# Gated attention and an MLP mixer in one kernel: z^T from overlapping transposes, the second token weight kept in row order, stores on the GpSimd queue

## The chip, the cores and the metric

The kernel runs on one core of one Trainium2 chip. A core has a matmul engine (TensorE, PE in the profile), three engines for elementwise work (VectorE is DVE, ScalarE is ACT, GpSimd is POOL), and SyncE (SP), which here only issues DMAs. SP and POOL each issue to a DMA queue of their own, in order; an instruction that waits holds all that stands behind it on its engine. The metric is the device time of one execution in microseconds; lower is better.

## The reference

There are 8 batches of 3008 rows. The first stage is attention with a squared ReLU and a gate, the second a mixer over tokens and then over channels. `z` is the query and the key at once, so the scores are symmetric.

```python
scores = z @ z^T / S                     # S = 3008, z: [S, 64]
attn   = maximum(scores, 0) ** 2
x      = u * (attn @ v)                  # u, v: [S, 256]
h      = maximum(x^T @ w_tok1, 0) @ w_tok2     # w_tok1: [S, 256], w_tok2: [256, S]
x2     = x + h^T
out    = x2 + maximum(x2 @ w_ch1, 0) @ w_ch2   # w_ch1: [256, 1536]
```

Inputs and the output are float32; the kernel computes in bfloat16 with float32 sums.

## The kernel before, in words

**Tiles.** The 3008 rows of a batch are 24 tiles of 128 (the last has 64 rows), in 6 groups of 4 (`GK`); `q` counts groups as queries, 512 columns (`QW`), and `g` as keys. Rows are loaded so that a partition takes neighbouring rows of DRAM (`rows_of`: row p*t + i, t = 4 or 3, goes to partition p, tile i). All that is indexed by a row must follow this order.

**Attention.** `score_run` (L399) multiplies z^T with itself. A score needs only 64 rows of PE's array, so two of them run at once, in the lower and the upper half; for this z^T stands in both halves (`zTs[b]`, partitions 0 to 63 and again 64 to 127). ACT takes the ReLU out of PSUM (`relu`, L437, L425) into an `at` tile, DVE squares it (`square` L445, `square_triangle` L473), and PE multiplies it with `v` into an accumulator (`av_matmul`, L533). As scores are symmetric, a block made once serves twice: SP turns it by DMA transpose (`flip` L492 into `fl`, `flip_tiles` L485 within a diagonal block). The 64 rows of the last tile also take half the array ("tails", `do_tails`). Between matmuls of 64 and of 128 rows PE changes its tiling. When a query group is done, `gate` (L628, L633) multiplies the accumulator with u^T into `xT`, and SP turns that into `x` (L640).

**Mixer.** While batch b + 1 is in attention, batch b goes through the mixer, in pieces: `tok1` (L675), `tok2` (L692; its sum is added to `xT` by DVE, L698), `turn_u2` (L708), `ch1` (L729; ReLU on ACT L742 or on DVE L744, into `h2pre`), `ch2` (L771; the residual sum L784 or L801 on DVE into `res`, which has three buffers, and then the store L788 or L804). The last groups of two batches share one ch2 piece, for which POOL copies parts of `h2pre` into `hs` (L749).

**z^T before.** For the next batch POOL loads each of the 6 groups into a `zs` tile (`load_z`, L113, cast to bfloat16), copies it doubled into `zr` (`turn_z`, L125) and SP transposes `zr` into `zT` (L126). For the first batch DVE doubles; groups 0, 1 and, later, 4 and 5 are turned on PE (`turn_late_z`), 2 and 3 by DMA.

**w_tok2 before.** Its columns must be in the order of the tiles. POOL loads a stretch into a staging tile (`load_w_tok2`) and copies it, with a step, into place (`order_w_tok2`, L220), once.

**Who sets the order.** The kernel writes out its order by itself: at build time a planner walks through PE's time with assumed costs (`push(engine, ready, busy, latency, ...)`), picks between scores, an attention group ("av") and a mixer piece, and emits every instruction on its engine in that order. `ring` models three PSUM slots that scores and pieces share, `at_group(n, f)` hangs a load or a transpose on the n-th key group. So a changed cost or rule of choice changes the order on all engines. The semaphores follow from the tiles: a load into a tile waits for the last reader of the tile that had the buffer before.

Of the kernel before, what the change touches and what calls it, by code (L numbers as in the profile page):

```python
# [13 lines left out]
P = 128  # L14
# [30 lines left out]
class Piece:  # L45


    def __init__(self, cost, needs, fn, opens=False, closes=False, room=None):
        self.cost, self.needs, self.fn = cost, needs, fn
        self.opens, self.closes, self.room = opens, closes, room  # L50


@with_exitstack
def kernel(
# [23 lines left out]
    NG = KT // GK  # L78
    widths = [min(QW, S - q * QW) for q in range(NQ)]
# [15 lines left out]


# [13 lines left out]
    def load_z(b, c):  # L110
        zs = sb.tile([P, GK, d_qk], BF16, tag="zs", name="zs", bufs=6)
        n = full_tiles[c]
        nc.gpsimd.dma_start(out=zs[:, :n, :], in_=rows_of(z[b], c))  # L113
        if n < GK:
            for r in range(2):
                nc.gpsimd.dma_start(
                    out=zs[r * TAIL:(r + 1) * TAIL, n, :], in_=last_rows(z[b]))
        loading(LOAD / 4)
        return zs

    def turn_z(zs, zT, c, engine, tag="zr", bufs=2):


        zr = sb.tile([P, GK, 2, d_qk], BF16, tag=tag, name="zr", bufs=bufs)
        engine.tensor_copy(zr[:], zs.unsqueeze(2).to_broadcast([P, GK, 2, d_qk]))  # L125
        nc.sync.dma_start_transpose(  # L126
            out=zT[:, c * GK:c * GK + GK, :], in_=zr.rearrange("p t h d -> p (t h d)"))
# [77 lines left out]
    def load_w_tok2(c):  # L205
        st = sb.tile([P, DT, QW], BF16, tag="h2", name="ws", bufs=ROOM["h2"])
        W = widths[c]
        nc.gpsimd.dma_start(
            out=st[:, :, :W],
            in_=moe_w_tok2.rearrange("(tc t) s -> t tc s", t=P)[:, :, c * QW:c * QW + W])  # L210
        ws[c] = st
        live["h2"] += 1
        loading(LOAD)

    def order_w_tok2(c):
        st = ws.pop(c)
        live["h2"] -= 1
        W, n = widths[c], full_tiles[c]
        for h in range(DT):
            nc.gpsimd.tensor_copy(  # L220
                w_tok2_sb[:, h, c * QW:c * QW + n * P].rearrange("p (t s) -> p t s", s=P),
                st[:, h, :n * P].rearrange("p (s t) -> p t s", t=n))
        if n * P < W:
            nc.gpsimd.tensor_copy(
                w_tok2_sb[:, :, c * QW + n * P:c * QW + W], st[:, :, n * P:W])

# [15 lines left out]
    zTs, vs, urs, uTs, xTs, xs, ws = {}, {}, {}, {}, {}, {}, {}  # L242
# [9 lines left out]

    LAST = NG - 1

# [126 lines left out]
    def score_run(us, start):  # L381
        slots = sorted((d for d in ring if d.t is not None), key=lambda d: d.t)
        for unit in us:
# [12 lines left out]
            for r, i, c0, c1 in parts(unit):  # L396
                k = g * GK + i
# [713 lines left out]
```

## Time and profile before

| what | value |
|---|---|
| median of 6 runs | 1170.46 us (1169.62 to 1172.18) |
| the profiled execution | 1170.25 us, span 1168.5 us |
| PE busy | 1159.3 us, 99% of the span |
| DVE, ACT, POOL busy | 541.1, 521.4, 161.0 us |
| DMA queue of SP and its kind (q1) | 131.74 MB, 53.6% of 16 engines' span |
| DMA queue of POOL (q0) | 32.32 MB, 20.2% |
| stores on SP | 105, of which 87 of 256 KB; median 2.2 us from issue to landing |
| loads of v, u, z on POOL | median 5.0, 5.1 and 4.8 us to landing |

PE is the engine to look at: where it never stands still, other engines' work costs nothing. A matmul is drawn with its whole way through the array, about 0.38 us for 512 columns, while the next starts 0.216 us after it; so PE's share says little on small losses, and those are read from start to start. Idle time of another engine matters only where PE waits for what that engine makes.

### The profile page before, as it was taken

What the parts mean: (1) busy time and instruction counts of PE and PEld (TensorE: products, weight loads), DVE (VectorE), ACT (ScalarE), POOL (GpSimd) and SP (SyncE); (2) the same over time, 40 slices, a digit from 0 to 9 for tenths busy, and PEclk for the clock granted to TensorE, in tenths of its full rate; (3) what the DMA queues carried; (4) which work ended last, traced back from release to release, by engine and by line L of the source; (5) the groups of instructions that cost most, each with busy time, mean ns of one, the idle gap of its engine ahead of it and who ended that gap; (6) DMA issues with size and microseconds to landing.
All of it is one profiled execution on the core that took longest, in us unless ns stands there. A gap on an engine that the chain in (4) does not pass through costs nothing.

```text
span 1168.5 us, 17791 instructions
## 1 busy us (share of the span) xinstructions
PE 1159.3 (99%) x7049; PEld 629.6 (54%) x7049; DVE 541.1 (46%) x819; ACT 521.4 (45%) x650; POOL 161.0 (14%) x328
## 2 busy tenths in 40 slices
PE   9999999999999999999999999999999999999998
PEld 3334554655546555555555655465454655555666
DVE  5785653355333563435634355242552336512544
ACT  7886443244442363343524435344454344513221
POOL 4372001102012100120101210101201000000000
PEclk9999999999999999999999999999999999999999
DMA  9999737797497965997858985798666977532121
GB/s 170 183 148 201 176 92 148 163 189 132 117 167 152 170 130 134 146 178 149 144 132 162 163 155 124 139 184 151 123 144 142 185 146 151 121 100 58 50 82 64
DMA packets 472883, 165.57 MB, mean 142 GB/s; under 512 B 436640, under 2 KB 450528, under 8 KB 472800
## 3 DMA queue, kind: packets, MB, share of 16 engines
q1 hardware_dynamic: 444944, 131.74, 53.6%
q0 software_dynamic: 27344, 32.32, 20.2%
q8 instruction: 55, 0.90, 0.3%
q10 hardware_dynamic: 512, 0.38, 0.1%
q14 instruction: 28, 0.23, 0.1%
HBM read 65.40 MB, written 24.64 MB: 77 GB/s over the span
## 4 chain that ended last, share of the span: by engine, by line
PE 96%; DMA 2%; ACT 1%; DVE 1%; issue 0%; SPq 0%; POOL 0%; ACTq 0%; DVEq 0%
PE acc L533 41%; PE op L771 21%; PE hp L729 21%; PE sc L399 6%; PE a_ps L675 3%; PE h_ps L692 3%; ACT at L437 1%; DMA fl<-at 1%; DMA at<-at 1%; DMA zf<-in_z_dram 0%; DMA v_sb<-in_v_dram 0%; DVE xT L698 0%; SPq L485 0%; DVE xT L628 0%; DVE h2pre L744 0%
## 5 line engine op out<-in xcount | busy, mean ns | idle before, releaser
L742 ACT ACTIVATE h2pre<-hp 128x1024 bf16<-128x1024 f32 (+1 forms) x191 | 191.0, 1006 | 364.6 <-PE hp L729 363.4
L533 PEld LDWEIGHTS <-v_sb 128*128 128x128 bf16 (+1 forms) x2304 | 209.4, 97 | 267.7 <-issue 65.7
L533 PE MATMUL acc<-at,v_sb 128*128 128x512 bf16 (+3 forms) x1464 | 350.9, 378 | 2.2 <-DVE xT L628 1.4
L437 ACT ACTIVATE at<-sc 128x1024 bf16<-128x1024 f32 (+1 forms) x284 | 272.0, 1024 | 159.1 <-PE sc L399 154.8
L445 DVE TENSOR_TENSOR at<-at 128x1024 bf16<-128x1024 bf16 (+1 forms) x284 | 200.1, 713 | 175.0 <-ACT at L437 174.8
L729 PE MATMUL hp<-xT,w_ch_sb 128*128 128x512 bf16 (+1 forms) x1152 | 266.7, 375 | 0.0
L771 PE MATMUL op<-w_ch_sb,h2pre 128*128 128x256 bf16 x2208 | 258.4, 273 | 0.3 <-DVE xT L698 0.2
L771 PEld LDWEIGHTS <-h2pre 128*128 128x128 bf16 x2208 | 216.0, 98 | 46.1 <-issue 0.5
L533 PE MATMUL acc<-fl,v_sb 128*128 128x512 bf16 (+1 forms) x840 | 199.9, 371 | 0.0
L729 PEld LDWEIGHTS <-w_ch_sb 128*128 128x128 bf16 x1152 | 112.7, 98 | 126.7 <-issue 0.2
L784 DVE TENSOR_TENSOR res<-op,u_sb 128x512 f32<-128x512 f32 x87 | 60.1, 691 | 206.5 <-PE op L771 206.5
L744 DVE TENSOR_SCALAR h2pre<-hp 128x1024 bf16<-128x1024 f32 (+1 forms) x97 | 117.3, 1209 | 52.1 <-PE hp L729 51.1
L628 DVE TENSOR_TENSOR xT<-acc,uT 128x512 bf16<-128x512 f32 (+1 forms) x96 | 63.2, 665 | 113.8 <-PE acc L533 113.6
L399 PE MATMUL sc<-zT 64*128 64x512 bf16 (+1 forms) x732 | 94.9, 360 | 0.5 <-ACT zT L986 0.2
L425 ACT ACTIVATE at<-sc 128x512 bf16<-128x512 f32 (+3 forms) x164 | 59.2, 446 | 68.0 <-PE sc L399 67.8
L125 POOL COPY zr<-zs 128x512 bf16<-128x512 bf16 x42 | 26.9, 640 | 398.7 <-DMA zT<-zr 392.4
L473 DVE TENSOR_TENSOR at<-at 128x512 bf16<-128x512 bf16 (+3 forms) x164 | 44.3, 323 | 59.4 <-ACT at L425 59.4
L399 PEld LDWEIGHTS <-zT 64*128 64x128 bf16 x732 | 31.3, 94 | 56.9 <-issue 39.8
L698 DVE TENSOR_TENSOR xT<-xT,h_ps 128x1024 bf16<-128x1024 bf16 (+1 forms) x48 | 55.6, 1192 | 6.4 <-PE h_ps L692 6.3
L168 POOL DMA_DIRECT2D v_sb<-in_v_dram x48 | 25.9, 546 | 146.2 <-PE acc L533 144.5
L675 PE MATMUL a_ps<-x_sb,w_tok_sb 128*128 128x256 bf16 x384 | 44.7, 273 | 0.0
L692 PE MATMUL h_ps<-w_tok_sb,a_sb 128*128 128x512 bf16 (+1 forms) x192 | 44.5, 374 | 0.1
(43 smaller groups left out, 210.8 us busy)
## 6 DMA issues: line engine op xcount, KB each, us to landing
out_dram<-res SPq DMA_DIRECT2D x87, 256.0 KB, 2.2
v_sb<-in_v_dram POOLq DMA_DIRECT2D x40, 256.0 KB, 5.0
ur<-in_u_dram POOLq DMA_DIRECT2D x40, 256.0 KB, 5.1
zs<-in_z_dram POOLq DMA_DIRECT2D x35, 64.0 KB, 4.8
at<-at SPq DMA_TRANSPOSE x123, 2.4
fl<-at SPq DMA_TRANSPOSE x105, 3.9
v_sb<-in_v_dram POOLq DMA_DIRECT2D x8, 192.0 KB, 6.3
ur<-in_u_dram POOLq DMA_DIRECT2D x8, 192.0 KB, 6.0
```

Of the source, the lines that this page charges most:

```text
L399: nc.tensor.matmul(sc[:, r, c0:c1], zT[h, k * P:(k + 1) * P], zT[h, q * QW + c0:q * QW + c1], start=True, stop=True)
L437: nc.scalar.activation(view, sv, ACT.Relu, scale=inv_S)
L445: nc.vector.tensor_mul(view, view, view)
L533: nc.tensor.matmul(o, vs[blk.b, g][rows, i, dh * P:(dh + 1) * P], rhs, start=first, stop=stop, skip_group_check=True)
L628: nc.vector.tensor_mul(xT[:, dh, :full * P].rearrange("p (t s) -> p t s", s=P), acc[:, :full * P].rearrange("p (t s) -> p t s", s=P), uT[: ...
L675: nc.tensor.matmul(st["a_ps"][:, th, :], w_tok1_sb[:, k, th * P:(th + 1) * P], x[:, :, i, :], start=(k == 0 and th == 0), stop=(k == KT - ...
L692: nc.tensor.matmul(h[:, dh, :W], st["a"][:, th, dh * P:(dh + 1) * P], w_tok2_sb[:, th, q * QW:q * QW + W], start=(th == 0), stop=(th == 1))
L729: nc.tensor.matmul(hp[:, r, :W], w_ch1_sb[:, dc, cc * P:(cc + 1) * P], xT[:, dc, :W], start=(dc == 0), stop=(dc == DT - 1))
L742: nc.scalar.activation(h2[:, :, :W], hp[:, :, :W], ACT.Relu)
L744: nc.vector.tensor_single_scalar(h2[:, :, :W], hp[:, :, :W], 0.0, AX.max)
L771: nc.tensor.matmul(op[:, i, :], h2, w_ch2_sb[:, cc, :], start=(cc == 0 and (i == 0 or apart)), stop=(cc == CHT - 1), skip_group_check=True)
L784: nc.vector.tensor_add(res.rearrange("p i (h d) -> p i h d", d=P), op.rearrange("p i (h d) -> p i h d", d=P), us[:, :, half * 2:half * 2 + ...
```

## The change

1. **z^T.** `zs` becomes one tile for a whole batch, with an empty tile of zeros at either end. SP transposes half a batch at a time, twice, once from tile k and once from tile k + 1 on, 128 columns (two tiles of z) to a block; so a block of `zT` has tile k - 1 in the lower and tile k in the upper half, and the score picks its block by the half (`z_tile`). POOL's doubling copy goes. The six z loads of a batch come in row order, with a turn three key groups after the third and after the sixth.
2. **w_tok2.** It is loaded straight into place in DRAM's order; the staging tiles and POOL's copies go. The add after `tok2` reads its PSUM sum with a step of 4 (or 3) elements to bring it into the order of the tiles; in the last group it is two adds.
3. **Stores** go to POOL's queue, but for the last pieces of the last batch (the other branch), which stay on SP.
4. **The planner.** SP's costs are 1.8 us for a flip and 1.2 us for each triangle piece; stores book nothing on SP. Scores wait (`together`) when the last block's tails will be ready soon, so that both go in one stretch of 64-row matmuls. The late z tiles of the first batch become mixer pieces marked `urgent`.

```diff
+    zs = consts.tile([P, KT + 2, d_qk], BF16)
...
     def load_z(b, c):
-        zs = sb.tile([P, GK, d_qk], BF16, tag="zs", name="zs", bufs=6)
         n = full_tiles[c]
-        nc.gpsimd.dma_start(out=zs[:, :n, :], in_=rows_of(z[b], c))
+        k = c * GK + 1
+        nc.gpsimd.dma_start(out=zs[:, k:k + n, :], in_=rows_of(z[b], c))
...
-    def turn_z(zs, zT, c, engine, tag="zr", bufs=2):
-        zr = sb.tile([P, GK, 2, d_qk], BF16, tag=tag, name="zr", bufs=bufs)
-        engine.tensor_copy(zr[:], zs.unsqueeze(2).to_broadcast([P, GK, 2, d_qk]))
+    def turn_z(zT, half):
+        n = KT // 2
+        for k in (half * n, half * n + 1):
+            nc.sync.dma_start_transpose(
+                out=zT[:, k:k + n:2, :],
+                in_=zs[:, k:k + n, :].rearrange("p t d -> p (t d)"))
+        if half:
+            nc.sync.dma_start_transpose(
+                out=zT[:, KT, :], in_=zs[:, KT:, :].rearrange("p t d -> p (t d)"))
...
+    def z_tile(b, half, k):
+        return k + 1 - half if b else k
...
     def load_w_tok2(c):
-        st = sb.tile([P, DT, QW], BF16, tag="h2", name="ws", bufs=ROOM["h2"])
+        cols = slice(c * QW, c * QW + widths[c])
         nc.gpsimd.dma_start(
-            out=st[:, :, :W],
-            in_=moe_w_tok2.rearrange("(tc t) s -> t tc s", t=P)[:, :, c * QW:c * QW + W])
+            out=w_tok2_sb[:, :, cols],
+            in_=moe_w_tok2.rearrange("(tc t) s -> t tc s", t=P)[:, :, cols])
-    def order_w_tok2(c):
...
-                k = g * GK + i
+                k = z_tile(b, r, g * GK + i) * P
+                m = z_tile(b, r, q * GK) * P
                 nc.tensor.matmul(
-                    sc[:, r, c0:c1], zT[h, k * P:(k + 1) * P],
-                    zT[h, q * QW + c0:q * QW + c1], start=True, stop=True)
+                    sc[:, r, c0:c1], zT[h, k:k + P], zT[h, m + c0:m + c1],
+                    start=True, stop=True)
...
-            done = push("sp", t, 2.45, 6.5, lambda t: flip(b, q, g, at, uses, done),
+            done = push("sp", t, 1.8, 6.5, lambda t: flip(b, q, g, at, uses, done),
...
-            for j, busy in ((0, 0.55), (1, 0.4)):
+            for j, busy in ((0, 1.2), (1, 1.2)):
...
-        done = push("sp", t, 0.3, 5.5, lambda t: blocks.update(
+        done = push("sp", t, 1.2, 5.5, lambda t: blocks.update(
...
             def add(t):
                 xT = xTs[b, q]
-                nc.vector.tensor_add(xT[:, :, :W], xT[:, :, :W], h[:, :, :W])
+                n = full_tiles[q]
+                to = xT[:, :, :n * P].rearrange("p h (t s) -> p h t s", t=n)
+                nc.vector.tensor_add(
+                    to, to, h[:, :, :n * P].rearrange("p h (s t) -> p h t s", t=n))
+                if n * P < W:
+                    to = xT[:, :, n * P:W]
+                    nc.vector.tensor_add(to, to, h[:, :, n * P:W])
...
-                    nc.sync.dma_start(
+                    nc.gpsimd.dma_start(
                         out=rows_of(out[b], q)[:, half * 2:half * 2 + 2, :],
...
+                    queue = nc.sync if b == B - 1 else nc.gpsimd
...
-                        nc.sync.dma_start(out=to, in_=res[r, j, :])
-                free["sp"] = max(free["sp"], t) + 0.4
+                        queue.dma_start(out=to, in_=res[r, j, :])
...
-                at_group(base + 3 * NG + j, lambda b=b, c=c, h=held: ask_z(b, c, h))
-                at_group(base + 3 * NG + j + 3, lambda b=b, c=c, h=held:
-                         turn_next_z(b, c, h.pop(c)))
+                at_group(base + 3 * NG + j, lambda b=b, j=j: load_z(b + 1, j))
+                if j % 3 == 2:
+                    at_group(base + 3 * NG + j + 3, lambda b=b, j=j: turn_next_z(b, j // 3))
...
-    def turn_late_z(c):
+    def late_z(c, landed):
+        zr = []
+        def turn(end):
+            take_slot()
+            zp = psum.tile([P, GK, P], F32, tag="ps", name="zp", bufs=3)
+            turn_on_pe(zr[0], zp)
...
+        cast = push("dve", landed, 0.42, 0.55, lambda t: zr.append(double_first_z(c)))
+        heads.append(Piece(0.23, [cast], turn, urgent=True))
...
+        together = (
+            blk is not None and blk.q > 1 and blk.b < B - 1 and not blk.tails
+            and blk.slot == 0 and t + 0.3 < tails_ready(blk) < FAR)
-        if n_now and ts <= t + NOW and (whole or (low and n_now >= 2)):
+        if n_now and not together and ts <= t + NOW and (whole or (low and n_now >= 2)):
             pick = "scores"
...
+        elif tm <= t + NOW and pieces[0].urgent:
+            pick = "mixer"
```

## The prediction

> **What bounds the kernel now.** I read the page's busy shares first, then the waits of PE, then PE's order of time around one wait and one ordinary stretch, and last the rows that the edits touch.
>
> ```profile
> span 1168.5 us, 17791 instructions
> PE 1159.3 (99%) x7049; PEld 629.6 (54%) x7049; DVE 541.1 (46%) x819; ACT 521.4 (45%) x650; POOL 161.0 (14%) x328
> ...
> PEclk9999999999999999999999999999999999999999
> DMA  9999737797497965997858985798666977532121
> ```
> PE is busy from end to end at the full clock; the other engines are half idle. What PE waits for (the view of waits, PE alone) is nearly nothing:
>
> ```profile
> PE acc L533 <- DVE xT L628: 1.4, 2, 1.2
> PE wp L157 <- DVE zero L892: 1.2, 1, 1.2
> PE acc L533 <- DMA v_sb<-in_v_dram: 0.6, 1, 0.6
> PE zp L149 <- DVE zr L143: 0.4, 2, 0.2
> ```
> Reading: us in total, times, longest. The view counts from the modelled end of a matmul. From start to start, the idle that exceeds the usual step adds up to about 5.3 us after the first 5 us: 1.1 ahead of 11.67 us, 0.3 at 14.6, 0.3 each at 39.4 and 52.4 (a score waits for a PSUM slot), 1.9 at 105.6 to 108, 0.65 at 1097, 0.26 at 1159, the rest in bits. That is the pool from which any edit that hides work can draw. The one other loss is the change between matmuls of 64 and of 128 rows (timeline of PE):
>
> ```profile
> 43.17 0.81 PE L399 MATMUL sc<-zT 64*128 64x512 bf16 x6
> 43.91 2.33 PE L533 MATMUL acc<-at,v_sb 128*128 128x512 bf16 x10
> 46.17 0.82 PE L399 MATMUL sc<-zT 64*128 64x512 bf16 x6
> ```
> Ten full matmuls step by 0.2158 us (2.158), yet 2.26 us pass from 43.91 to 46.17; three pairs of halves need 0.647 and 0.74 pass. So each change of row count costs 0.10 us, a stretch of halves 0.20.
>
> **The change, part by part.** PE's 7049 matmuls keep their number and shapes; only their order moves.
>
> *Order of scores and tails.* Listing both orders, the stretches of 64-row matmuls fall from 140 to 136: 4 x 0.20 = -0.8 us, certain as far as the order is. Scores that are held back for the tails come a half group (4 x 0.2158 = 0.86 us) or two later; what waits for them, ACT and then PE some groups on, is covered by the blocks already made, else it costs that much.
>
> *z^T.* 42 Pool copies (26.9 us) and 42 of the 44 zT transposes go; 35 come (5 in each of 7 batches: four of 768 columns, one of 128). Blocks of 128x128 are 24 a batch before and 25 after, so DMA work stays. SP issues one transpose in a median 1.217 us: 7 fewer, -8.5 us of SP. None lies on PE's path: z^T is turned ten of a batch's 36 key groups ahead of use (some 36 us of about 130). Worth 0; if that cover were gone, a half batch would cost one transpose's 3.5 us to landing. On SP the turn can wait for its z loads (4.8 us to land, asked three key groups, at least 3 x 8 x 0.2158 = 5.2 us, earlier); behind it stand the attention flips, whose users are PE.
>
> *Second token weight.* 13 Pool copies (11.3 us, once, off the path) go. The 48 adds now read PSUM with a step of 16 bytes; the last q splits in two. These are the rows (by form):
>
> ```profile
> L698 DVE TENSOR_TENSOR xT<-xT,h_ps 128x1024 bf16<-128x1024 bf16 x40 | 47.3, 1214 | 6.4 <-PE h_ps L692 6.3
> L698 DVE TENSOR_TENSOR xT<-xT,h_ps 128x896 bf16<-128x896 bf16 x8 | 8.6, 1080 | 0.0
> L220 POOL COPY w_tok_sb<-ws 128x512 bf16<-128x512 bf16 x10 | 9.2, 948 | 0.5 <-DMA ws<-in_moe_w_tok_dram 0.5
> L125 POOL COPY zr<-zs 128x512 bf16<-128x512 bf16 x42 | 26.9, 640 | 398.7 <-DMA zT<-zr 392.4 <-DMA zs<-in_z_dram 6.0
> ```
> No strided PSUM read is in the trace. From below: (1214-1080)/128 = 1.05 ns an element, so the add already goes one element at a time and gains nothing from neighbours; stride free, price 0 (a gain is excluded, since nothing gets shorter). From above, the nearest strided row, Pool's stepped copy against its plain one: 948/640 = 1.48, or +0.58 us an add. The Trainium skill speaks against the edit: "Advanced Engine Details and Errata", PSUM Cachelines, has lines of 8 bytes and wants every two consecutive elements contiguous, or matmuls slow down. If a DVE read were halved likewise, an add would take about 1024 x 1.05 = 1.07 us more. I take the DVE row, price 0: PE writes this PSUM at 512 columns in 0.2158 us, 0.84 ns for a pair, so one pair in each 1.05 ns is less than what the memory is seen to do. That is an inference, and both upper ends go into the range. The second add of the last q costs about 0.13 us (fixed part of 1214 - 1024 x 1.05), 8 times; only in the last batch, where the adds run with nothing beside them, does PE see it.
>
> *Stores on Pool.* 100 of 105 stores leave SP (0.333 us each, 33 us) for Pool (546 ns a load, so 55 us): Pool goes from 161 to about 178 us, still 15%. A store waits for its DVE sum, and SP was held for 195.6 us that way (its waits, below); the flips no longer stand behind that. On Pool the loads of u, v, z and the hs copies now do. Until now Pool ran ahead of the schedule as far as buffers let it, and had long waits of its own:
>
> ```profile
> SPq L788 <- DVE res L784: 195.6, 56, 16.2
> SPq L189 <- DMA ur<-in_u_dram: 38.4, 7, 11.5
> POOL v_sb L168 <- PE acc L533: 144.5, 22, 23.2
> ```
> In the new order loads are asked at their planned place: u three groups (5.2 us or more) ahead of its transpose against 5.1 us to land, v at least six groups ahead of use. SP waited 38.4 us for u already, and PE lost nothing by it. The skill is against this edit too: "DMA: Bandwidth & Descriptors", Issuing engine by pattern, sends plain stores to Sync, with a first byte at 0.6 us against 1 us on Pool. By the rule a store lands 0.4 us later, by the rows up to 2.8 us (2.2 on SP; 5.0 for Pool's loads of the same 256 KB). Either is hidden: of the three res buffers each comes round after 5 us or more in all but three cases of the trace, and the kernel's last stores stay on SP. I take 0, bounds -0.5 and +2 us.
>
> *Schedule.* The costs booked for SP become 1.8 us for a flip and 1.2 for a triangle's pieces (before 2.45, 0.55, 0.4, 0.3); the trace has 1.652 and 1.195, so the new due times are truer. What untrue ones cost shows in the chain:
>
> ```profile
> 97.60 6.04 DMA fl<-at
> ...
> 104.67 1.03 ACT at L437
> ...
> 106.33 1.29 DVE xT L628 x2
> ...
> 107.66 0.37 PE acc L533
> ```
> One flip landed in 6.04 us instead of the median 3.9, its at buffer came free late, ACT and the DVE behind it were late, and the gate L628 held the accumulator: 1.9 us of PE. Stores had no part (none before 141 us), so whether it goes depends on the order alone: -1.0, between -1.9 and 0. At the start the late z tiles are turned one piece earlier. The 0.3 at 14.6 goes, but the 1.1 us ahead of 11.67 stay in another place, since the first matmul on the second v tile waits for its landing: -0.4 (0 to -1.2). One of the two 0.3 us bubbles at 39 and 52: -0.3. Last batch, split add and order of the pieces behind it: +0.4. New small waits where h2pre moves (DVE gets 9 more of them, ACT 9 fewer): +0.3 (0 to 2).
>
> **Sum.** -0.8 - 1.0 - 0.4 - 0.3 + 0.4 + 0.3 = -1.8 us. The profiled execution took 1170.25 us (span 1168.5 and 1.75 around it), 0.2 below the median of 1170.46, so 1168.4 there and 1168.6 as a median.
>
> **Rivals.**
> *A, slower: the strided sum.* DVE is half idle on average, but not where the adds run (windows around them; third pair is DVE, of the window's length):
>
> ```profile
> 116.00:128.00 12.00, 11.94 (x60) 4.92 (x60) 9.72 (x13) 5.02 (x9) 0.00 (x0) 1.00 1.10 196
> 543.00:552.00 9.00, 9.00 (x53) 4.44 (x51) 7.04 (x10) 2.81 (x4) 0.04 (x1) 1.00 0.97 214
> 680.00:695.00 15.00, 15.00 (x83) 7.08 (x82) 12.54 (x18) 6.23 (x10) 4.06 (x8) 1.00 0.88 144
> ```
> Room is 2.3, 2.0 and 2.5 us, 2.2 on average, for six adds. At +1.07 a batch needs 6.3 and PE, waiting for PSUM slots, loses 4.1: 8 x 4.1 = 33, 1202 us. At Pool's +0.58, 8 x (3.5 - 2.2) = 10, 1179 us. Below +0.37 an add it is hidden. Against it: the slope of the two rows.
>
> *B, slower: Pool's order.* A v load that waits for PE (6.6 us on average above) holds the stores behind it; with three res buffers the fourth sum stops DVE, and so the squares. From four sums inside one such wait on; at about 5 us in half of seven batches, +17, 1186 us. Against it: in the listing the v loads stand ahead of the stores, and PE's groups that free them mostly follow each other with no mixer piece between.
>
> *C, faster: relief of SP.* Without stores and late sums between them all flips land early: the whole 1.9 and both bubbles go and nothing new comes, 1166.8 us. For it: 195.6 us of SP's waits. Against: PE hardly felt them.
>
> *D: nothing.* The stall at 105 stays and new waits eat the switches: 1170.
>
> **Numbers.** 0.2% is 2.3 us, about what a measurement of this kernel can tell from no change (six runs spread over 2.6 us). Forecast 0.52 (0.24 of it over 2.3 us faster, 0.28 within), C 0.14 (faster), D 0.10 (within), A 0.16, B 0.08 (both slower). So faster 0.38, same 0.38, slower 0.24. The forecast alone spans 1166.8 to 1170.5; the range for 8 in 10 reaches A at Pool's price: 1166.5 to 1180.
>
> **What would show it.** Right: 136 stretches of halves; the add's row near 1214 ns; no PE wait at h_ps beyond 1 us in all; Pool near 178 us; the PE wait on xT near 106 us smaller or gone. Wrong: an add at 1.6 us or more with PE waiting for xT at h_ps and hp (A); DVE res waiting on DMA out_dram (B); SP waiting longer for u or z loads with PE waiting on at or fl (the loads' cover gone).

## The result: 0.8% slower

The changed kernel takes 1179.99 us in the median, beside 1171.4 for the kernel before on the same chip: a ratio of 1.0081 (95% interval 1.0057 to 1.0105). Here and below a ratio leaves out the executions more than 1.5% above the fastest of the same kernel (three of 17 here, up to six of 20, in e3), while medians and counts take all, so that in e1, e3, e5, e6 and e8, where most are left out, the median shows more of the loss. The profiled execution took 1174.39 us (span 1172.6). The 16 others go from 1175.47 to 1193.05 us, and the longer ones are those whose mean granted clock is lower: 1175.5 us at 0.997 to 0.998, 1181 at 0.995 to 0.997, 1191 to 1193 at 0.991.

The page of the changed kernel:

```profile
span 1172.6 us, 17778 instructions
PE 1160.7 (99%) x7049; PEld 629.8 (54%) x7049; DVE 545.2 (46%) x836; ACT 515.2 (44%) x641; POOL 182.7 (16%) x375
...
PEclk9999999999999999999999999999999999999999
DMA  9999658968597957997679866897769866632122
```

Nothing in it looks different: 99% PE, a 9 for the clock in every slice. The loss is a few single stops, too short for slices of 29 us whose 9 means 90% or more. The waits of PE find them (us in total, times, longest):

```profile
PE sc L401 <- DMA zT<-zs: 5.3, 3, 3.9
PE wp L175 <- DVE zero L902: 1.2, 1, 1.2
PE acc L535 <- DVE xT L630: 0.8, 1, 0.8
```

A new first line: a score waits for z^T. Before, the first line was the gate's wait of 1.4, and no wait on a transpose of zT stood in the list. The timeline of PE around the longest one:

```profile
619.15 1.89 PE L535 MATMUL acc<-fl,v_sb 128*128 128x512 bf16 x8
620.98 0.39 PE L535 MATMUL acc<-at,v_sb 64*128 64x512 bf16 x2
621.20 0.27 PE L401 MATMUL sc<-zT 64*128 64x128 bf16 x2
625.41 0.45 PE L401 MATMUL sc<-zT 64*128 64x512 bf16 x4 [3.93 <-DMA zT<-zs]
625.78 5.31 PE L535 MATMUL acc<-fl,v_sb 128*128 128x512 bf16 x16
```

From 621.20 to 625.41 PE stands still. And what follows is slow as well: 8 matmuls take 1.89 us ahead of the stop (at 619.15), 16 take 5.31 us behind it, where 3.6 would be expected. The windows before, just after and later say why; the number after the five engines is the granted clock:

```profile
617.20:621.20 4.00, 4.00 (x20) 1.68 (x20) 0.00 (x0) 0.00 (x0) 0.00 (x0) 1.00 1.01 143
625.40:629.00 3.60, 3.59 (x14) 1.43 (x15) 1.09 (x4) 1.43 (x4) 0.00 (x0) 0.67 0.70 150
630.00:634.00 4.00, 4.00 (x21) 1.86 (x19) 1.38 (x2) 1.02 (x1) 0.23 (x1) 0.99 0.28 64
```

Eight matmuls behind the stop step by 0.43 us instead of 0.2158: the trace has the clock at half from 626.64 to 630.05 us, 3.41 us, which costs another 1.7. The one wait is worth 4.1 + 1.7 = 5.8 us.

The chain of waits shows what the score waited for:

```profile
613.89 1.21 SPq L130
615.10 0.05 issue
615.15 10.21 DMA zT<-zs
625.36 0.05 issue
625.41 0.44 PE sc L401 x2
```

The second transpose of the half batch is issued at 615.15 and needs 10.21 us to land, and the score starts 0.05 us later. Meanwhile Pool's timeline has a store, a load of u and four of v, which took 6.4 to 8.9 us to land themselves:

```profile
613.87 0.59 POOL L797 DMA_DIRECT2D out_dram<-res  x1 [2.95 <-DVE res L793]
614.45 0.55 POOL L197 DMA_DIRECT2D ur<-in_u_dram  x1
614.97 1.09 POOL L186 DMA_DIRECT2D v_sb<-in_v_dram  x2
616.01 1.10 POOL L189 DMA_DIRECT2D v_sb<-in_v_dram  x2
```

From start to start, against the usual step, the profile's account is: stop and half clock at 621, +5.8; a score's waits at 479 (1.0) and 86 (0.7), +1.7; the 1.9 at 105 gone, two bubbles of 0.3 gone, four changes fewer (-0.8): +4.2 in all, and the span grew by 4.1.

### The profile page after: what moved, and what is told of

It is laid out like the page before. It is cut to its first block, busy times and chain, and to the rows that moved or that the text cites. A ratio compares the mean times of both kernels' runs of the same rounds, so it can differ in the third digit from the quotient of the medians.

```text
span 1172.6 us, 17778 instructions
## 1 busy us (share of the span) xinstructions
PE 1160.7 (99%) x7049; PEld 629.8 (54%) x7049; DVE 545.2 (46%) x836; ACT 515.2 (44%) x641; POOL 182.7 (16%) x375
## 4 chain that ended last, share of the span: by engine, by line
PE 93%; DMA 3%; SPq 1%; DVE 1%; issue 1%; ACT 0%; POOL 0%; DVEq 0%
PE acc L535 39%; PE op L780 21%; PE hp L738 21%; PE sc L401 6%; PE a_ps L677 4%; PE h_ps L694 3%; DMA zT<-zs 2%; DMA ur<-in_u_dram 1%; SPq L130 1%; ACT at L439 0%; DMA uT<-ur 0%; DMA zf<-in_z_dram 0%; DVE xT L703 0%; SPq L207 0%; POOL v_sb L186 0%
## 5 line engine op out<-in xcount | busy, mean ns | idle before, releaser
L751 ACT ACTIVATE h2pre<-hp 128x1024 bf16<-128x1024 f32 (+1 forms) x182 | 183.0, 1008 | 339.4 <-PE hp L738 333.8
L447 DVE TENSOR_TENSOR at<-at 128x1024 bf16<-128x1024 bf16 (+1 forms) x284 | 194.1, 688 | 192.8 <-ACT at L439 191.7
L753 DVE TENSOR_SCALAR h2pre<-hp 128x1024 bf16<-128x1024 f32 (+1 forms) x106 | 127.1, 1199 | 68.2 <-PE hp L738 68.2
L797 POOL DMA_DIRECT2D out_dram<-res x87 | 47.7, 548 | 600.4 <-DVE res L793 600.3
```

The lines of the kernel that those rows point to most:

```text
L447: nc.vector.tensor_mul(view, view, view)
L751: nc.scalar.activation(h2[:, :, :W], hp[:, :, :W], ACT.Relu)
L753: nc.vector.tensor_single_scalar(h2[:, :, :W], hp[:, :, :W], 0.0, AX.max)
```

## The experiments

All kernels were timed in five rounds beside the kernel before on the same chip. One number is given beside the ratio: in how many executions the mean granted clock was below 0.9985. Profiles without a longer stop stand at 1.000. One stretch of half clock of 3.41 us, as in the profile above, takes 0.0015 off the mean, so an execution below 0.9985 has probably had two or more, and one at 0.991 six. The changed kernel had 15 of its 17 below. In the four sets the kernel before had 25 of 57, 15 of 32, 15 of 39 and 24 of 59 of them.

The two theories at first: Z, z^T arrives with no lead over its first score; S, the stores on Pool's queue delay the loads behind them.

**e1: z^T six key groups earlier, in all batches.**

```diff
-            at_group(base + 3 * NG, lambda b=b: new_zT(b + 1))
+            at_group(base + 2 * NG, lambda b=b: new_zT(b + 1))
...
-                at_group(base + 3 * NG + j, lambda b=b, j=j: load_z(b + 1, j))
+                at_group(base + 2 * NG + j, lambda b=b, j=j: load_z(b + 1, j))
...
-                    at_group(base + 3 * NG + j + 3, lambda b=b, j=j: turn_next_z(b, j // 3))
+                    at_group(base + 2 * NG + j + 3, lambda b=b, j=j: turn_next_z(b, j // 3))
```

> The changed kernel with its z loads and turns six key groups (one query group, some 20 us) earlier; nothing else differs but what the planner makes of it. Theory Z (the half-batch turns took away the lead of z^T: its first half landed 0 to 4 us before the first score, where it was 4 to 9 us, and a late one also halves the matmul clock): PE waits for zT vanish, 1167 to 1171 us, runs close together. Rival S (stores in the loads' queue delay u, z and v and slow the transposes, whatever their lead): still 1176 to 1182 us, with waits for other tiles.

Measured: 1178.04 us, ratio 1.002 (0.9995 to 1.0045), 21 of 22 executions below 0.9985. Its profile (waits of PE) has lost most of the wait on zT and has another in its place, at 104 us:

```profile
PE sc L401 <- ACT at L439: 4.8, 3, 4.2
...
PE sc L401 <- DMA zT<-zs: 0.4, 1, 0.4
```

The ratio is nearly back. In the first batch the z loads and turns now stand wholly in the stretch where the weights are loaded: all five turns took 11 to 24 us to land (3 to 21 in the changed kernel). The stop at 104 us stands behind an `x` transpose whose issue took 4.9 us and a flip that landed in 6.4. Z holds for the wait, the median missed its band.

**e2: z^T as before** (Pool's doubling copy, a transpose for each key group), all else changed.

```diff
-    def turn_z(zT, half):
+    def turn_z(zs, zT, c, engine, tag="zr", bufs=2):
...
-                    at_group(base + 3 * NG + j + 3, lambda b=b, j=j: turn_next_z(b, j // 3))
+                at_group(base + 3 * NG + j + 3, lambda b=b, c=c, h=held:
+                         turn_next_z(b, c, h.pop(c)))
```

> The changed kernel with the z path of before (six doubled groups by GpSimd copies and six transposes a batch), all else changed. Z: 1167 to 1171 us. S: 1176 to 1182 us.

Measured: 1176.79 us, ratio 1.0002 (0.9969 to 1.0034), 8 of 14 below 0.9985. The profiled execution has a span of 1165.3 and no wait over 1.2 us; other executions reach 1186. So the z path carries the loss in the ratio. The median of all executions is still above before's, so something in the rest still makes executions that stop.

**e3: the stores back on SP**, all else changed.

```diff
-                    nc.gpsimd.dma_start(
+                    nc.sync.dma_start(
                         out=rows_of(out[b], q)[:, half * 2:half * 2 + 2, :],
...
-                    queue = nc.sync if b == B - 1 else nc.gpsimd
+                    queue = nc.sync
...
+                free["sp"] = max(free["sp"], t) + 0.4
```

> The changed kernel with all stores back on the Sync queue (0.4 us booked for each, as before). Z: the waits for zT stay, 1176 to 1185 us. S: 1168 to 1172 us.

Measured: 1187.82 us, ratio 1.0075 (1.0048 to 1.0102), 20 of 20 below 0.9985. S falls: taking the stores off Pool cures nothing. The waits of PE have a z^T wait and a longer one, behind transposes of `u_sb` and `fl` that landed in 15 to 16 us:

```profile
PE sc L401 <- DVE res L793: 10.4, 1, 10.4
PE sc L401 <- DMA zT<-zs: 5.4, 2, 2.8
```

But both waits on zT are in batch 1, at 86 to 93 us. In batches 2 to 7 the turns landed in 2.3 to 4.0 us and no score waited for one; the long stop, from 574 to 585 us, is more than 40 us from any turn. So this is not the stop of the changed kernel.

**e4: the kernel before with the new z path alone.**

```diff
+    zs = consts.tile([P, KT + 2, d_qk], BF16)
...
+    def turn_z(zT, half):
...
+                k = z_tile(b, r, g * GK + i) * P
+                m = z_tile(b, r, q * GK) * P
```

> The kernel before with the half-batch z turns alone. Z: waits for zT at the heads of batches, 1174 to 1185 us. S: 1170 to 1172 us, since the stores stay on the Sync queue.

Measured: 1182.34 us, ratio 1.0077 (1.0058 to 1.0097), 14 of 14. The z path alone gives the size of the whole loss. But its profile stops elsewhere than at zT:

```profile
PE sc L414 <- DVE res L799: 10.1, 3, 9.0
```

In batches 2 to 7 every turn landed in 2.3 to 4.6 us and no score waited for zT. What PE waited for was DVE's sum, which waited for a `u_sb` transpose:

```profile
853.62 14.18 DMA u_sb<-xT
```

The nearest turns of z^T are at 756 to 767 and at 909 to 919 us, so it was not they that held this transpose up. Beside it are loads. From 842.5 to 857.1 us Pool asked 16 of u, z and v; the last of them:

```profile
853.22 0.56 POOL L193 DMA_DIRECT2D ur<-in_u_dram  x1 [0.92 <-DMA ur<-in_u_dram]
855.01 1.06 POOL L182 DMA_DIRECT2D v_sb<-in_v_dram  x2 [1.23 <-DMA zs<-in_z_dram]
856.06 1.07 POOL L185 DMA_DIRECT2D v_sb<-in_v_dram  x2
```

Before, ten loads of the same stage came at 838 to 848 us, and then Pool stood before its doubling copies, which waited 392.4 us in all for `zr` to come free. Without the copies Pool runs ahead until it needs a free v buffer:

```profile
POOL v_sb L182 <- PE acc L548: 409.9, 23, 76.5
```

(144.5 before.) So the z path can do harm in two ways: the half batch arrives when it is needed, and without the copies the loads come bunched, and transposes among them land late. Counted over the traces from 120 us on (most loads that Pool asked within 15 us; transposes of SP that took over 8 us to land):

| kernels | loads within 15 us | late transposes |
|---|---|---|
| before, e10 (copies) | 11 | 7 to 8 |
| e2, e7, e9, e11, e13 to e15 (copies and stores) | 9 | 7 to 12 |
| e3, e4 (neither) | 16 | 20 to 25 |
| changed, e5, e8, e12 (stores, z^T in parts) | 13 to 14 | 17 to 23 |
| e1, e6, e16 (the same, z^T earlier) | 7 to 8 | 8 to 12 |

The next runs were planned before this count, with L, the lead alone (which is Z), and J, that the half batches' own transposes jam SP's queue. The count speaks for bunched loads in J's place, but no run changes the bunching alone: that it is the cause is not shown.

**e5: the lead bought on the other side**, with later scores.

```diff
-            turned[b + 1, c] = Done(pe[0] + 10.0)
+            turned[b + 1, c] = Done(pe[0] + 16.0)
...
-            turned[b + 1, NG // 2 - 1] = Done(pe[0] + 10.0)
+            turned[b + 1, NG // 2 - 1] = Done(pe[0] + 16.0)
```

> The changed kernel, but the planner is told that a half batch of z^T is ready 16 us after its turn instead of 10, so the next batch's first scores come later in PE's order; no DMA moves of its own. Theory L (the lead of z^T over the first score is lost, nothing else): PE's wait on zT falls from 12 us to under 1 us and the ratio to before is 0.998 to 1.003, about 1169 to 1175 us. Theory J (the half batch's big transposes, issued back to back beside the loads of u and v, jam SP's queue, and flips and u_sb behind them come late too): the wait on zT goes, but waits of 4 us or more on DVE or ACT behind late transposes stay, ratio 1.004 to 1.010, 1176 to 1183 us.

Measured: 1197.09 us, ratio 1.0151 (1.01 to 1.0202), 6 of 6. Both bands missed, on the bad side. PE's waits:

```profile
PE acc L535 <- DMA at<-at: 6.6, 4, 3.1
...
PE sc L401 <- DMA zT<-zs: 1.0, 1, 1.0
```

The wait on zT went from 5.3 to 1.0, as L says, but scores made later leave the `at` blocks no lead over their users, and PE stops there. The lead between scores and use has no slack to give to z^T. This is the only run that gives z^T lead and leaves the loads bunched (14 within 15 us), and it gains nothing.

**e6: z^T six groups earlier, but not for batch 1**, so not in the crowded start.

```diff
-            at_group(base + 3 * NG, lambda b=b: new_zT(b + 1))
+            z0 = base + (2 if b else 3) * NG
+            at_group(z0, lambda b=b: new_zT(b + 1))
...
-                at_group(base + 3 * NG + j, lambda b=b, j=j: load_z(b + 1, j))
+                at_group(z0 + j, lambda b=b, j=j: load_z(b + 1, j))
...
-                    at_group(base + 3 * NG + j + 3, lambda b=b, j=j: turn_next_z(b, j // 3))
+                    at_group(z0 + j + 3, lambda b=b, j=j: turn_next_z(b, j // 3))
```

> The changed kernel with the z loads and turns of batches 2 to 7 six key groups (some 20 us) earlier; batch 1's stay where they are, out of the crowded start. Theories L and J both: wait on zT under 1 us except in batch 1 (0.7 us, as in the changed kernel), ratio to before 0.996 to 1.001, 1167 to 1172 us; it may beat both kernels by the 105-us stall and the 136 stretches. If the loss came from elsewhere (stores on Pool, the strided sum, the planner): 1176 to 1182 us, ratio 1.005 to 1.010.

Measured: ratio 1.0007 (0.9973 to 1.0041); median 1178.43, 8 of 14 below 0.9985; profiled span 1168.0. The ratio is inside the band, the median, with five executions of 1187 us and more, outside. The wait on zT is 1.7 us, once, at the second half of batch 6, whose turn SP issued 18 us behind the first.

**e7: only the sum by stride and the stores**, with z^T and the planner of before.

```diff
+                to = xT[:, :, :n * P].rearrange("p h (t s) -> p h t s", t=n)
+                nc.vector.tensor_add(
+                    to, to, h[:, :, :n * P].rearrange("p h (s t) -> p h t s", t=n))
...
-                    nc.sync.dma_start(
+                    nc.gpsimd.dma_start(
                         out=rows_of(out[b], q)[:, half * 2:half * 2 + 2, :],
...
-                free["sp"] = max(free["sp"], t) + 0.4
```

> The kernel before with two parts of the change alone: the second token weight in row order with its sum read by stride, and the stores on Pool's queue (nothing booked on SP for them); z path and planner's rules as before. Theories L and J: these two cost nothing, ratio to before 0.997 to 1.002, 1167 to 1174 us, add near 1170 ns, no wait of PE on h_ps. Theory S (stores delay the loads on Pool's queue) or a dear strided sum: ratio 1.004 to 1.010, 1176 to 1183 us.

Measured: 1167.74 us (1166.73 to 1169.69), ratio 0.993 (0.9904 to 0.9957), 0 of 11 below 0.9985. Better than any theory gave, and steady. The groups by form show the add with the step of 16 bytes (ns of one after the second bar's first number):

```profile
L685 DVE TENSOR_TENSOR xT<-xT,h_ps 128x1024 bf16<-128x1024 bf16 x40 | 47.4, 1215 | 1.6 <-PE h_ps L677 1.5
L685 DVE TENSOR_TENSOR xT<-xT,h_ps 128x768 bf16<-128x768 bf16 x8 | 7.6, 947 | 0.0
L689 DVE TENSOR_TENSOR xT<-xT,h_ps 128x128 bf16<-128x128 bf16 x8 | 2.2, 281 | 0.0
```

1215 ns against 1214 in row order before. The stride is free; the split costs 947 + 281 - 1080 = 0.15 us each.

**e8: z^T in thirds.**

```diff
-        n = KT // 2
+        n = KT // 3
...
-        if half:
+        if half == 2:
...
-                if j % 3 == 2:
-                    at_group(base + 3 * NG + j + 3, lambda b=b, j=j: turn_next_z(b, j // 3))
+                if j % 2 == 1:
+                    at_group(base + 3 * NG + j + 3, lambda b=b, j=j: turn_next_z(b, j // 2))
```

> The changed kernel with z^T turned in thirds (two overlapping transposes of four blocks each, after the second, fourth and sixth load) instead of halves of six blocks; 7 zT transposes a batch instead of 5. The first two groups are asked one key group sooner and in a smaller burst. Theory L: the lead grows by some 4 us, wait on zT 0 to 3 us in all, ratio 0.999 to 1.005, 1170 to 1177 us. Theory J: the burst of four is cut to two, so landings above 7 us get rarer as well, ratio 0.997 to 1.003. If neither matters, as the changed kernel, 1.006 to 1.010.

Measured: 1181.94 us, ratio 1.0023 (0.9993 to 1.0053), 10 of 14 below 0.9985. The profile is not cured:

```profile
PE sc L401 <- DMA zT<-zs: 11.4, 4, 4.7
```

Two of its four waits are stops of 3.8 and 4.9 us, and one of 3.0 is in batch 1; at 335 and 338 us two turns land in 11.5 and 8.9 us, among four v loads that land in 11 to 12. Asking one group sooner does not give enough lead, and a smaller burst does not help beside those loads. Inconclusive between L and J.

The better version being found in e7, the next set splits it and the planner's part.

**e9: the stores on Pool alone** (the part of e7's diff that concerns stores).

> The kernel before with its stores on Pool's queue and nothing else (nothing booked on SP for them). The kernel with the stores and the strided sum was 0.993 of before. Theory Q (the stores relieve SP's queue, so flips no longer stand behind late sums and the rare stall of 4 us or more with its half clock gets rarer): all of that gain is here, ratio 0.991 to 0.997, 1165 to 1170 us. Theory W (the gain comes from the strided sum: Pool's 13 copies gone, other order at the start): nothing here, ratio 0.998 to 1.003.

Measured: 1167.64 us (1167.01 to 1169.67), ratio 0.9956 (0.9942 to 0.9969), 0 of 17 below 0.9985, where the kernel before had 15 of 39. Theory Q's band: the whole gain is the stores'. Its profiled execution has a span of 1165.3 us, and no wait of PE over 1.2. The stall at 105 us is gone, though PE's order is the same as before up to 808 us. Pool's timeline around it, before:

```profile
96.02 0.53 POOL L179 DMA_DIRECT2D ur<-in_u_dram  x1 [10.01 <-DMA uT<-ur]
96.54 1.08 POOL L113 DMA_DIRECT2D zs<-in_z_dram  x2
97.58 1.09 POOL L116 DMA_DIRECT2D zs<-in_z_dram  x2
109.05 0.57 POOL L179 DMA_DIRECT2D ur<-in_u_dram  x1 [10.38 <-DMA uT<-ur]
```

and with the stores on Pool:

```profile
84.50 1.11 POOL L179 DMA_DIRECT2D ur<-in_u_dram  x2
139.96 0.56 POOL L788 DMA_DIRECT2D out_dram<-res  x1 [54.34 <-DVE res L784]
```

The first store waits 54 us for its sum and holds all loads behind it. Before, Pool had run ahead and asked five loads at 96 to 98 us, just when the flip of 97.60 us was on its way that then landed late. The stores are a brake on the loads, as the doubling copies were. That the brake removed the stall is read from the two traces; e14 below has the brake and a stop at the same place.

**e10: the planner's part alone** on the kernel before.

```diff
-            done = push("sp", t, 2.45, 6.5, lambda t: flip(b, q, g, at, uses, done),
+            done = push("sp", t, 1.8, 6.5, lambda t: flip(b, q, g, at, uses, done),
...
-        if n_now and ts <= t + NOW and (whole or (low and n_now >= 2)):
+        if n_now and not together and ts <= t + NOW and (whole or (low and n_now >= 2)):
...
+        elif tm <= t + NOW and pieces[0].urgent:
+            pick = "mixer"
```

> The kernel before with the planner's part alone: 1.8 and 1.2 us for SP's transposes, scores held back for the tails, the late z tiles of the first batch as urgent pieces; z path, second token weight and stores as before. Theory P (with the new costs and rule the blocks are made with less lead, so a late transpose reaches PE): the kernel with all but the z path was 1.000 of before while the sum and the stores alone gave 0.993, so the planner's part costs about 0.7%: ratio 1.003 to 1.010. Theory N (the planner's part is neutral, the two ratios of different chips differ by chance): 0.997 to 1.003, stretches 136, stall at 105 us gone.

Measured: 1182.87 us, ratio 1.0066 (1.0035 to 1.0098), 12 of 12. Theory P. The stall of the first batch is not gone but five times as long. The chain ahead of its end:

```profile
100.70 2.04 SPq L495
...
104.18 9.01 DMA fl<-at
...
116.20 0.61 PE sc L402 x2
```

A flip issued at 104.18 lands after 9.01 us. At 103.5 to 106.2 us Pool had asked one u and four z loads, the same five as before at 96 to 98. PE's timeline and the clock of the window behind it:

```profile
102.70 2.32 PE L536 MATMUL acc<-at,v_sb 128*128 128x512 bf16 x10
114.37 0.61 PE L402 MATMUL sc<-zT 64*128 64x512 bf16 x2 [9.35 <-ACT at L440]
```

```profile
114.50:118.50 4.00, 3.39 (x11) 0.87 (x9) 3.78 (x7) 4.00 (x5) 0.00 (x0) 0.50 1.14 255
```

**e11: e7's kernel once more.**

> The kernel with the sum by stride and the stores on Pool alone, once more, beside the other parts on one chip: again 0.991 to 0.997 of before, about 1168 us, if its gain is real; 0.998 to 1.003 if it was chance of the chip or of before's runs.

Measured: 1167.2 us, ratio 0.9962 (0.9946 to 0.9978), 1 of 17. The gain is real; against e9 on the same chip the sum by stride adds nothing.

**e12: the changed kernel without the planner's part** (e4's edit and e7's).

> The changed kernel with the planner of before: z^T by half batches, the sum by stride, the stores on Pool. Theory P: against the changed kernel's 1.008 the planner's share is gone, 0.998 to 1.004, some 1170 to 1177 us, with the loss of the z path (1.0077 alone, on SP-stored outputs) partly made up by the stores. Theory N: as the changed kernel, 1.005 to 1.010. A wait of PE on zT, or on DVE and ACT behind jammed transposes, of 4 us or more is seen in either.

Measured: 1191.19 us, ratio 1.0154 (1.0115 to 1.0193), 6 of 6. Above both bands. The parts do not add up: the planner's part costs 0.7% on the kernel before, yet with half batches of z^T it saves as much. The wait is the known one:

```profile
PE sc L399 <- DMA zT<-zs: 14.5, 4, 7.4
```

The last four runs ask which piece of the planner costs, on top of e9, and whether the lead alone cures e12.

**e13: SP's costs.**

```diff
-            done = push("sp", t, 2.45, 6.5, lambda t: flip(b, q, g, at, uses, done),
+            done = push("sp", t, 1.8, 6.5, lambda t: flip(b, q, g, at, uses, done),
...
-            for j, busy in ((0, 0.55), (1, 0.4)):
+            for j, busy in ((0, 1.2), (1, 1.2)):
...
-        done = push("sp", t, 0.3, 5.5, lambda t: blocks.update(
+        done = push("sp", t, 1.2, 5.5, lambda t: blocks.update(
```

> Before with the stores on Pool (0.9956 of before, 1167.6 us), and of the planner's part only SP's costs: 1.8 us for a flip, 1.2 for each triangle piece. Theory P1 (the cheaper flip makes the planner use a flipped block too soon, so a late transpose reaches PE): 1.000 to 1.007 of before, 1172 to 1181 us. If the costs are neutral: 0.994 to 0.998, 1166 to 1170 us.

Measured: 1169.82 us, ratio 0.998 (0.9965 to 0.9996), 2 of 22, at the upper edge of the neutral band: perhaps 0.2% worse than the stores alone, though the two were timed in different sets and their intervals just touch.

**e14: scores held back for the tails.**

```diff
+        together = (
+            blk is not None and blk.q > 1 and blk.b < B - 1 and not blk.tails
+            and blk.slot == 0 and t + 0.3 < tails_ready(blk) < FAR)
...
-        if n_now and ts <= t + NOW and (whole or (low and n_now >= 2)):
+        if n_now and not together and ts <= t + NOW and (whole or (low and n_now >= 2)):
```

> Before with the stores on Pool, and of the planner's part only the rule that holds scores back for the tails. Theory P2 (held-back scores make at blocks later, the lead over PE shrinks): 1.000 to 1.007 of before. If neutral: 0.993 to 0.998, fewer than 140 stretches of 64-row matmuls, each 0.2 us.

Measured: 1168.03 us, ratio 0.9963 (0.9942 to 0.9984), 3 of 22: neutral. It has 140 stretches of 64-row matmuls in its trace, so by itself the rule does not merge any. The traced execution is one of the three at low clock (1175.3 us), and it has the stall of the first batch, longer than before:

```profile
PE a_ps L675 <- ACT at L437: 3.6, 1, 3.6
```

PE stands from 104.66 to 108.60 us and again from 109.36, in e9's order of work up to there and with the stores on Pool. The last `w_ch` and u loads were asked at 86 to 88 us instead of e9's 83 to 85 and took 10 to 13 us, and the flip issued at 94.99 took 9.3. So the brake makes this stall rarer (no e9 execution of 17, at most three of 22 here) but does not exclude it.

**e15: the late z tiles as urgent pieces.**

```diff
-    for c in range(GK, NG):
-        at_group(c - GK + 1, lambda c=c: turn_late_z(c))
...
+    late_z(4, 7.8)
+    late_z(5, 9.0)
...
+        elif tm <= t + NOW and pieces[0].urgent:
+            pick = "mixer"
```

> Before with the stores on Pool, and of the planner's part only the first batch's late z tiles as urgent mixer pieces. Theory P3 (the first batch's whole order shifts against the crowded DMA there, which is where the kernel with the planner's part alone stood still for 9.5 us at 105 us): 1.000 to 1.007 of before, with a stall between 80 and 120 us. If neutral: 0.994 to 0.998.

Measured: 1175.88 us, ratio 1.001 (0.998 to 1.0039), 11 of 14: this piece is most of the planner's cost, some 0.5% over e9. PE's waits and the chain that leads there:

```profile
PE a_ps L677 <- ACT at L439: 6.0, 1, 6.0
```

```profile
101.33 3.83 SPq L494
...
105.26 1.25 SPq L642
...
106.60 3.91 DMA fl<-at
```

One flip's issue is stuck in SP until 105.16, and the flip behind it, which PE needs, is issued at 106.60 only. The loads that it shares the DMA with (`w_ch` and u, at 92 to 95 us) are those that e9 asks at 83 to 85. So two late tiles at 8 us shift the order of the first batch, and some 90 us on a flip meets loads that had been out of its way. The traced execution of e14 has the same meeting without the late tiles, so they make it common (11 of 14) rather than possible; that it is the cause is read from these traces, not tested by itself.

**e16: e12 with z^T earlier from batch 2 on** (e6's edit).

> The changed kernel with the planner of before (1.0154) and the z loads and turns of batches 2 to 7 six key groups earlier. Theory L (what z^T by half batches costs is its lead and nothing else): wait on zT from 14.5 us to under 2, ratio 0.995 to 1.000, 1167 to 1172 us; it may tie with the stores alone. If the half batch's transposes cost by jamming SP wherever they stand: 1.003 to 1.012, 1176 to 1187 us.

Measured: 1173.31 us, ratio 0.999 (0.9966 to 1.0014), 7 of 14, from e12's 1.0154. The half batches do not cost wherever they stand, as the rival had it. The remaining wait on zT is that of batch 1, which was not moved (86.64 to 90.57 us):

```profile
PE sc L399 <- DMA zT<-zs: 3.9, 2, 3.6
```

But the move gives z^T lead and at the same time takes the turns out of the bunch: in batches 2 to 7 they landed in 2.3 to 6.3 us, where e12 had up to 14.1, and at most 7 loads were asked within 15 us, where e12 had 13. So it does not tell the lead from the loads. Even so it does not reach the stores alone (0.9956), so getting rid of Pool's doubling copies brought nothing.

## Why the prediction was wrong, step by step

It said 1168.6 us and faster or the same; the kernel is 0.8% slower. The range to 1180 just held the median, for a reason that was not among its cases.

- **z^T: the step that failed.** Its cost was put at 0, with "turned ten of a batch's 36 key groups ahead of use (some 36 us of about 130)" as the cover. That counted from the turn to the batch's end. But the first scores of a batch run well ahead of it: in the trace before, in batches 2 to 7, the first two key groups of z^T landed 4 to 9 us ahead of the first score, and that was all. A half batch is turned after its third load, 8 to 16 us later (for batch 3 at 333.4 instead of 324.8 us), and for that the lead was 0 to 4 us in these batches: batch 4 at 480.24 and 480.28 us, batch 5 at 625.36 and 625.41. The prediction named the price without cover, one landing of 3.5 us; the landings that mattered took 7.4 to 10.2 us, and the stop brought the half clock with it. The same step put the doubling copies at nothing, as work of Pool off PE's path: their 392.4 us of waiting had spaced the loads behind them. That the z path carries the loss is shown by e4 (the path alone, 1.0077) and e2 (put back, 1.0002, though its median stays 4 us above before's). That it can be turned without most of the loss is shown by e16 (0.999 from 1.0154), less firmly by e6 (1.0007, but a median of 1178.43). How the loss divides between the lead and the bunched loads stays open: e4's trace stops at a late `u_sb` and not at zT, the changed kernel's at zT, and no run moves one without the other but e5, which gains nothing. J, as it was put, is not borne out: the late transposes that PE waited for in e3 and e4 stand some 40 us and more from the nearest turn.
- **Stores on Pool.** Put at 0 with bounds of -0.5 to +2 us: outside the bounds, a gain of 0.44%, some 5 us (e9). In the profiled execution it is 3.2 us, 1168.5 to 1165.3; the rest is probably that no execution of e9 stops for longer. The page "DMA: Bandwidth & Descriptors" of the Trainium skill (Issuing engine by pattern; the first-byte times that the prediction took with it stand under Specifications), which wants plain stores on Sync, speaks against it; here a store on Pool does land later, in 2.7 us beside 2.2 on SP, and the kernel is faster.
- **The stall at 105 us.** Forecast to go, and it went, but for another reason. "Stores had no part (none before 141 us)" was the error: a store that has not run yet holds the queue from 85 to 140 us, and the loads held there are those that stood beside the late flip before. The order did not decide it: e9 has before's order and not the stall. e14 has the stores and the stall in one execution, so the loads held back are not the whole of it.
- **The planner.** Four stretches fewer came as said (136), 0.8 us, and so did -0.4 at the start (PE's losses from 5 to 60 us went from 2.8 to 2.4) and -0.3 for a bubble. What the sum left out is what the new order does later: the late z tiles cost 0.5% (e15), SP's truer costs perhaps 0.2% (e13). Costs that agree better with the trace did not make a better order.
- **The sum by stride.** Right: 0, by the slope of the two DVE rows; 1215 ns against 1214. Rival A is out. The rule on PSUM cachelines ("Advanced Engine Details and Errata"), taken as a price for DVE, would have been +1.07 us an add; the runs show 0.
- **Rival B** (Pool's order) is out: Pool waits 600 us for sums, and neither PE nor DVE waits for a store or a load of Pool's for more than 0.3 us. **Rival C** (relief of SP, 1166.8 us) is close to what the stores do alone, 1167.6; whether that gain is SP's relief or the brake on Pool's loads, no run separates.
- **"What would show it"** came near: PE waiting because cover is gone was named, but for at and fl behind loads of u or z that SP waits for. It came at zT, and SP waited less for u (19.6 us, before 38.4).

Best of all kernels: the stores on Pool's queue with all else as before, 0.9956 of before; with the sum by stride, 0.993 and 0.9962 in two sets.

What stays open: why the new planner helps the half batches (e12 against the changed kernel), and the shares of the lead and of the bunched loads. That stops and half clock also make the longer executions is inferred from their clock; only one execution of each kernel has a trace.

## To carry to other kernels

Before costing a later transfer at nothing, find the first instruction that reads it and measure the time from landing to that read, in each round; its planned place in the stage did not tell it here. Work that is taken off an idle engine can have paced what stands behind it: the copies' 392 us of waits were no cost, but they spaced the loads. Where a matmul engine is 99% busy, the cost of a late operand was the stop plus, for the longer stops, a stretch at half clock, and it came in some executions only, so look at the spread as well as at one profile. A queue's waiting instruction paces all that stands behind it: moving stores in among loads can hold back loads that ran too far ahead.

## What the runs showed of the hardware

- **Half clock after a stop.** In the clock records of all 18 traces the granted clock is full or half, nothing between, and inside the kernel a spell of half clock lasts 3.41, 6.83, 10.24 or 13.65 us: one to four times 3.41. Meanwhile matmuls of 512 columns step by 0.427 us instead of 0.2158, those of 448 by 0.373 instead of 0.189. Each stop of PE of 4 us or more was followed by one (4.1 us by 3.41; 4.4 to 10.6 us by 6.83 to 13.65), no single stop of up to 2 us was. Between them it went both ways, even within e8: a stop of 3.0 us was followed by 3.41 us of half clock, one of 3.8 us by none. A spell costs about half its length as far as PE has work in it. This agrees with the Trainium skill ("TensorE: Matmul & The Clock Gate", Part 1: a free-running window of some 3.4 us, and half clock after an idle one), but for the stop of 3.0 us, which was shorter than the window. The sum had left this out because the profile before had no single stop over 1.4 us.
- **A transpose's landing time is not a constant.** Of the same five z^T transposes in the changed kernel (landing times, minimum, median, maximum, in the window around batch 5):

```profile
DMA to landing us min/median/max: 2.3/5.5/10.2
```

The median of the half batches' transposes is 3.6 us, the longest 20.7, in the first batch. Those of over 8 us in batches 4 and 5 lie beside loads of v that land in 6.5 to 8.9 us themselves, those of e8 at 335 us beside loads of 11 to 12. A median from the page was used in the prediction where the tail decides.
- **SP issues a z^T transpose in 1.2 us, of 128 columns as of 768** (medians of 1225 and 1248 ns in the changed kernel), a flip in 1.65, but when the DMA is crowded it takes up to 11.3 us (a flip in e3) and 14.4 (a turn in e1): then the issue itself stays in the queue, and the next transpose starts that much later.
